# Whole token rows scattered into the experts' order, in place of a table of row numbers and gathers

## The chip, the cores and the metric

The kernel runs on one core of a Trainium2 chip. The metric is the device time of one execution in microseconds (us), median of several runs; for the kernel before it is 893.01 us (three runs: 884.34, 893.01, 897.72). Profiles come from one profiled execution each; TensorE is PE, VectorE is DVE, ScalarE is ACT, GpSimd is POOL, SyncE is SP.

## The reference

Attention, then a layer of eight experts. `q`, `k`, `v` are 8 batches x 8 heads x 576 tokens x 64. `q` and `k` are rotated, scores are scaled and go through a softmax, and the attention output is laid out as `x`, 4608 token rows of 512 values. Each token goes to one expert:

```
logits = x @ w_gate + modality_bias[modality_id]
e_idx = np.argmax(logits, axis=1)
gate_w = softmax(logits)[e_idx]
for e in range(8):
    mask = e_idx == e
    h = np.maximum(x[mask] @ w1[e], 0.0)          # 512 -> 1024
    out[mask] = gate_w[mask, None] * (h @ w2[e])  # 1024 -> 512
```

How many tokens an expert gets is known only when the kernel runs, so the rows of one expert have to be brought together.

## The kernel before, in words

**Attention** works on 32 pairs of heads (`NPAIR`), four pairs to a batch, b = n // 4 for pair n. For a pair the rotation takes four steps on POOL (`rope_`, parts 1, 0, 2, 4: lines 454 to 462) and one on ACT (part 3, which writes the high part), `swap` copies the halves of a head past each other with DMAs (L470), `scores`, `rowmin`, `expo`, `fill`, `evac`, `AV` and `outp` follow on PE, DVE and ACT. `load` brings the next q and k of a pair, 576 KB in each half, into one of two buffers.

**Routing.** After each fourth pair `xout` writes the batch's rows into `X` in DRAM, and `route` finds each token's expert, its gate and its place among the expert's tokens (`oi`). `scatter` (L727) then writes 8 bytes per token, its number and its gate (`VAL`), into the table `TAB` at row `oi`: five indirect DMAs of up to 128 rows a batch, issued by POOL.

**Experts.** Tokens are worked on in blocks of one expert: block 0 of 256 rows, eight superblocks of 512, one block of 256 and one of 128 (`slots`, `nt`), and up to 19 further blocks behind a branch. The first five blocks are planned from the first five batches alone (`plan0`, on POOL, during attention), the others from all eight (`plan`, on DVE, in small steps between those of superblocks 1 to 5, lists `POPS` and `late`). For a block `m_plan` reads expert and first row into SP's registers, `m_ix` loads the block's piece of the table twice (`ix` for the outputs, `xi` for the rows), and `m_gather` computes row numbers `iy` (L1000) and gathers the rows: one indirect DMA (L1013) brings 128 pieces of 512 bytes, so a superblock takes 16 and the whole run 148, all issued by POOL. Rows lie in four buffers `XG`, two of which are the memory of attention's `AT`. DVE transposes them (`m_tr`, L1058), `m_super` computes a superblock with seven products in place of eight (L1194), then the second layer (L1326), and `m_store` scatters the output rows (L1109). First weights come with `m_load1` (L1029), second with `m_load2` (L1034), on SP's queue; `m_split` and `m_wsplit` split them into a high and a low part.

**Order.** PE, ACT, DVE and POOL follow an order written out by hand: every step of attention has a key in `KEYS`, in units of us, which is added to 14.438 times the pair's number; `EDGE` gives other keys for single pairs, and `MOE` those of block 0 and of the first rows. Steps are issued in the order of their keys, each engine waits in that order for what it needs, and SP's queue keeps it as well until key `end` of the last pair (472.56). After that SP's order is set by the framework's scheduler, by when it expects things to be ready, and the other engines follow the program.

Of the kernel before, what the change touches and what calls it, by code (L numbers as in the profile page):

```python
# [18 lines left out]
P = 128  # L19
# [3 lines left out]
BLK = 256  # L23
# [5 lines left out]
NB_STATIC = 1  # L29

# [191 lines left out]
    rows=(5.189, -7.595, 2.778, 1.17, -0.984, 8.071, 5.429, 11.766, 15.341, 15.3411, 15.3412, 15.3413, 15.3414, 15.3415, 15.3416, 15.3417, 15.3418, 15.3419, 15.342, 15.3421, 15.3422, 15.3423, 15.3424, 15.3425),  # L222
# [3 lines left out]
AFTER = {(0, 3): (30, 'av', 0), (0, 4): (30, 'av', 0), (0, 5): (30, 'av', 1), (0, 6): (30, 'av', 1), (0, 7): (30, 'out', 1), (1, 0): (31, 'av', 0)}  # L226
# [4 lines left out]
def tile_attention_moe(ctx: ExitStack, tc: tile.TileContext, qk, v, mod, wg, mb, w1, w2, rope, cf, ci, out):  # L231
# [7 lines left out]
    X = dram.tile([N, DM], F32, name="X")  # L239
    TAB = dram.tile([(E + 1) * N, 2], I32, name="TAB")  # L240
# [11 lines left out]
    TOT = cst.tile([1, 1], I32, name="TOT")  # L252
    EPS = cst.tile([P, 1], F32, name="EPS")
# [111 lines left out]
    MI = rc.tile([P, B, 5, 2], I32, name="MI")  # L365
    WGT = rc.tile([P, DM // P, E], F32, name="WGT")
    MF = rc.tile([P, B, 5], F32, name="MF")
    BI = rc.tile([P, B, 5, E], F32, name="BI")
    MBB = rc.tile([P, 2, E], F32, name="MBB")
# [8 lines left out]
    def setup():  # L378
# [20 lines left out]
        TI = W1[0].rearrange("p a b -> p (a b)")[:, 0:(E + 1) * N * 2 // P].bitcast(I32)  # L399
        g.memset(TI, EMPTY)  # L400
        for t in XG[0:2]:
            g.memset(t, 0.0)
# [6 lines left out]
    def setdma(part):  # L409
# [10 lines left out]
        else:  # L420
            d(out=MBB.rearrange("p a e -> p (a e)"), in_=mb.rearrange("a e -> (a e)").unsqueeze(0).to_broadcast([P, 2 * E]))
            d(out=TAB.rearrange("(p r) w -> p (r w)", p=P), in_=TI)

    def setup2(part):
# [8 lines left out]
        else:  # L433
            BT = sm.tile([P, B * 5, E], F32, name="BT", tag="BT", bufs=1)
# [188 lines left out]
    def xout(b):  # L623
        Bt = bt_[b]
        xd = X[b * S:(b + 1) * S, :]
        nc.sync.dma_start(out=xd[0:512, :].rearrange("(p j) d -> p j d", j=4), in_=Bt["x"])
# [3 lines left out]


# [92 lines left out]
    def scatter(b, j):  # L724
# [3 lines left out]
            out=TAB, out_offset=bass.IndirectOffsetOnAxis(ap=oi[0:n, j:j + 1], axis=0),  # L728
            in_=VAL[0:n, b, j, :], in_offset=None, bounds_check=E * N - 1, oob_is_err=False).ins
# [7 lines left out]


# [5 lines left out]
    def plan0():  # L744
# [44 lines left out]
        cmp = t1("cmp", [NB_MAX, E])[:, 0:NSA + 1, :]  # L789
# [17 lines left out]
        G_.tensor_scalar(ge, nb, -float(SUP), float(N), op0=ALU.mult, op1=ALU.add)  # L807
        G_.tensor_tensor(cs, cs, ge.unsqueeze(1).to_broadcast(shs), op=ALU.mult)
        G_.tensor_tensor(hc, hc, EBv, op=ALU.add)
        G_.tensor_scalar(hc, hc, float(-E * N), None, op0=ALU.add)  # L810
# [4 lines left out]
        G_.tensor_scalar(rb[:, 0:1], rb[:, 0:1], float(E * N), None, op0=ALU.add)  # L815
# [3 lines left out]
        G_.tensor_copy(PLA[:, 1, 0:NA], rb)  # L819
# [5 lines left out]
        G_.tensor_scalar(EB9, sl[:, 0:E + 1], float(N), None, op0=ALU.mult)  # L825
        G_.tensor_scalar(EBN, EBv, float(-E * N), None, op0=ALU.add)
# [3 lines left out]
    def plan():  # L830
# [26 lines left out]
        def blocks(x, n, w, o, eo):  # L857
# [15 lines left out]
            V_.scalar_tensor_tensor(o[:, 1, 0:n], sl[:, 0:n], float(w), rb[:, 0:n], op0=ALU.mult, op1=ALU.add)  # L873
# [39 lines left out]
        yield  # L913
        V_.tensor_reduce(hr, hc, op=ALU.add, axis=AX.X)
        yield
        V_.tensor_scalar(pl[:, 1, ns:ns + 1], hr, float(E * N), None, op0=ALU.add)
# [778 lines left out]
```

## Time and profile before

| | |
|---|---|
| median of three runs | 893.01 us |
| profiled execution, time and span | 888.49 and 886.6 us |
| PE busy | 838.3 us, 95% of the span |
| DVE, ACT, POOL busy | 725.3, 622.3, 649.0 us |
| moved by DMA | 141.06 MB, 159 GB/s over the span |
| mean granted TensorE clock | 0.988 |

The span runs from the first to the last instruction. Attention fills it up to about 465 us, the experts the rest. A row of the table by stage gives the busy time of each engine in that stretch, the granted clock, the mean busy share of the 16 DMA engines, and their rate. Busy time of PE is modelled from pipelined matmuls; what counts here is its idle time and who ended it.

### The profile page before, as it was taken

What the parts mean: (1) busy time and instruction counts of PE and PEld (TensorE: products, weight loads), DVE (VectorE), ACT (ScalarE), POOL (GpSimd) and SP (SyncE); (2) the same over time, 40 slices, a digit from 0 to 9 for tenths busy, and PEclk for the clock granted to TensorE, in tenths of its full rate; (3) what the DMA queues carried; (4) which work ended last, traced back from release to release, by engine and by line L of the source; (5) the groups of instructions that cost most, each with busy time, mean ns of one, the idle gap of its engine ahead of it and who ended that gap; (6) DMA issues with size and microseconds to landing.
All of it is one profiled execution on the core that took longest, in us unless ns stands there. A gap on an engine that the chain in (4) does not pass through costs nothing.

```text
span 886.6 us, 24920 instructions
## 1 busy us (share of the span) xinstructions
PE 838.3 (95%) x9504; PEld 690.8 (78%) x9504; DVE 725.3 (82%) x1612; ACT 622.3 (70%) x1325; POOL 649.0 (73%) x507
## 2 busy tenths in 40 slices
PE   2899999999999999999989799999999998999995
PEld 2687777777777777777768689898989896989895
DVE  6788888898898988888878788989988986798562
ACT  2897989889898888887964467565646563646453
POOL 3899988988989989999358888886886865334111
PEclk9999999999999999999999999999999998999999
DMA  8766868878788786755847292244445321521330
GB/s 266 222 191 169 265 171 213 175 202 207 193 204 195 201 202 173 223 153 155 228 126 237 86 187 74 78 128 159 159 143 185 109 73 34 167 86 52 113 140 22
DMA packets 84346, 141.06 MB, mean 159 GB/s; under 512 B 27592, under 2 KB 54364, under 8 KB 83192
## 3 DMA queue, kind: packets, MB, share of 16 engines
q1 hardware_dynamic: 73624, 118.28, 49.2%
q0 software_dynamic: 9248, 19.46, 7.0%
q8 instruction: 77, 1.26, 0.6%
q10 hardware_dynamic: 1344, 1.62, 0.6%
q14 instruction: 53, 0.43, 0.2%
HBM read 104.61 MB, written 19.51 MB: 140 GB/s over the span
## 4 chain that ended last, share of the span: by engine, by line
PE 79%; DVE 7%; issue 5%; ACT 4%; POOL 4%; DMA 1%; POOLq 0%; SPq 0%; DVEq 0%; ACTq 0%
PE psY L1326 18%; PE ps L566 16%; PE ps L485 14%; PE psH L1194 12%; PE ps L508 9%; PE ps L601 3%; PE psY L1194 2%; PE ps L1079 1%; PE psH L1079 1%; PE psY L1098 1%; ACT P L503 1%; DVE X L1155 1%; POOL HL L462 1%; DVE W1L L442 1%; DMA SW<-HL 1%
## 5 line engine op out<-in xcount | busy, mean ns | idle before, releaser
L494 DVE CUSTOM_DVE_ANT_1 sc<-ps,ZERO 128x576 f32<-128x576 f32 x288 | 206.6, 749 | 24.8 <-PE ps L485 14.6
L503 ACT ACTIVATE P<-sc,mn 128x576 f32<-128x576 f32 x256 | 196.0, 769 | 5.7 <-DVE mn L494 5.1
L485 PE MATMUL ps<-HL 64*128 64x288 f32 x960 | 170.9, 312 | 14.9 <-ACT HL L445 10.7
L485 PE MATMUL ps<-SW 64*128 64x288 f32 x960 | 170.4, 313 | 5.8 <-DMA SW<-HL 5.6
L485 PEld LDWEIGHTS ps<-HL 64*128 64x128 f32 x960 | 136.5, 191 | 20.7 <-ACT HL L445 10.7
L485 PEld LDWEIGHTS ps<-SW 64*128 64x128 f32 x960 | 136.3, 191 | 10.2 <-issue 7.7
L566 PE MATMUL ps<-PH,AT 128*64 128x320 f32 (+1 forms) x1024 | 139.3, 414 | 2.1 <-DVE PH L541 1.9
L1194 PE MATMUL psH<-HL,W1H 128*128 128x256 f32 x576 | 123.3, 283 | 5.8 <-ACT TB L445 3.0
L1013 POOL DMA_INDIRECT XG<-X,iy x80 | 106.9, 1336 | 29.7 <-issue 20.7
L541 DVE COPY PH<-ps 128x512 f32<-128x512 f32 (+1 forms) x160 | 98.4, 631 | 14.3 <-PE ps L508 8.5
L445 ACT ACTIVATE PH<-ps 128x512 f32<-128x512 f32 (+1 forms) x160 | 85.3, 551 | 33.1 <-PE ps L508 23.1
L566 PEld LDWEIGHTS ps<-PH,AT 128*64 128x64 f32 x1024 | 68.3, 137 | 51.1 <-DVE PH L541 5.3
L1194 PE MATMUL psH<-HL,W1L 128*128 128x256 f32 x384 | 107.9, 281 | 0.0
L462 POOL TENSOR_TENSOR HL<-ST,HL 128x1152 fp32r<-128x1152 f32 x31 | 82.4, 2657 | 34.3 <-ACT HL L445 34.2
L508 PEld LDWEIGHTS ps<-idf,P 64*128 64x128 f32 x2304 | 86.7, 138 | 21.7 <-ACT P L503 9.2
L1326 PE MATMUL psY<-W2H,SW 128*128 128x512 f32 x256 | 102.0, 399 | 1.5 <-issue 1.5
L1013 POOL DMA_INDIRECT AT<-X,iy x68 | 88.2, 1297 | 20.4 <-issue 18.3
L1326 PE MATMUL psY<-W2L,SW 128*128 128x512 f32 x256 | 101.5, 396 | 0.7 <-issue 0.7
L508 PE MATMUL ps<-idf,P 64*128 64x64 f32 x2304 | 98.2, 225 | 3.7 <-ACT AT L445 1.6
L1194 PEld LDWEIGHTS psH<-HL,W1H 128*128 128x128 f32 x576 | 96.1, 190 | 7.1 <-ACT TB L445 3.2
L1109 POOL DMA_INDIRECT out_dram<-sc,ix x36 | 41.8, 1162 | 68.7 <-ACT sc L1108 60.6
L458 POOL TENSOR_TENSOR ST<-ST 128x1152 f32<-128x1152 f32 x30 | 79.6, 2653 | 1.2
(281 smaller groups left out, 1984.7 us busy)
## 6 DMA issues: line engine op xcount, KB each, us to landing
ST<-in_moe_w_dram SPq DMA_DIRECT2D x88, 512.0 KB
ST<-in_qk_dram SPq DMA_DIRECT2D x62, 576.0 KB
SW<-HL SPq DMA_DIRECT2D x124, 216.0 KB
AT<-in_v_dram SPq DMA_DIRECT2D x32, 256.0 KB
X<-X SPq DMA_DIRECT2D x8, 1024.0 KB
XG<-X,iy POOLq DMA_INDIRECT x80
AT<-X,iy POOLq DMA_INDIRECT x68
AT<-in_v_dram SPq DMA_DIRECT2D x64, 16.0 KB
```

Source lines behind the costliest of these rows:

```text
L445: return nc.scalar.activation(o, i, AF.Copy, scale=scale)
L458: e.tensor_tensor(a, a, b, op=ALU.add)
L462: e.tensor_tensor(d["HL"][:, 1, o], a, d["HL"][:, 0, o].bitcast(F32), op=ALU.subtract)
L485: nc.tensor.matmul(ps[:, g, 0:288], t[:, wq, q0:q0 + P], t[:, wk, k0:k0 + 288], start=(m == 0), stop=(m == len(L) - 1))
L494: nc.vector.tensor_tensor_reduce(sc, d.pop(("S", u))[:, :, 0:288], ZERO.unsqueeze(2).to_broadcast([P, 2, 288]), 1.0, FMAX, ALU.add, ALU.mi ...
L503: nc.scalar.activation(p, sc.rearrange("p a b -> p (a b)"), AF.Exp, bias=mn, scale=-1.0, accum_out=d["sum"][:, u:u + 1])
L508: nc.tensor.transpose(ps[:, g, c:c + 64], src[r, k0:k0 + P], idf[r, r])
L541: alone(d["at", f], g, (nc.vector.tensor_copy if g else acopy)(o, i).ins, int(f[1] in "23B"))
L566: i = nc.tensor.matmul(pa[hh * 64:hh * 64 + 64, 0:c1 - c0], d["V"][:, hh, kt, :], r, start=(kt == 0), stop=(kt == 4))
L1013: inst = nc.gpsimd.indirect_dma_start(out=x[:, t, g, :], out_offset=None, in_=X.rearrange("n (i f) -> (n i) f", f=P)[0:rows], in_offset=ba ...
L1194: nc.tensor.matmul(ps[b][:, r * BLK:r * BLK + BLK], w[:, c, f0:f0 + P], x[:, c, :], start=(first and r == 0 and c == 0 and i == 0), stop=( ...
L1326: nc.tensor.matmul(po[t], hx[:, c, o:o + P], w[:, c, :], start=(k == 0 and c == 2 * q and i == 0), stop=(k == 3 and c == 2 * q + 1 and i = ...
```

## The change

`X` rows get longer: 512 values, then token number and gate, in a pitch of 528 words. `vout` writes numbers and gates of a batch there, `back` loads 128 whole rows into one of two buffers `XL`, and `scatter` writes these whole rows to their place in `XS`, a DRAM array with room for each expert (`RS` rows) in which the experts' rows lie in order. `TAB`, the index arithmetic and all 148 gathers go; a block's rows are now plain transfers of `XS` on SP's queue, four for each 256 rows (`m_rows`), and `m_ix` is a single load of numbers and gates. `pads` writes a block of empty rows behind each expert's last row, once all tokens are counted, since a block may reach past them. `ZR` holds these empty rows; the tail of `XS` is filled at the start, as `TAB` was. Constants of routing move into memory of the `XG` buffers, the clearing of `XG` at the start and by ACT falls away, and in `plan` the first row of a block is limited with one more small instruction. Keys: the late places of the scatters of batches 4, 5 and 6 (pairs 19, 23 and 27) are dropped for those in `KEYS`, and `vout` and `back` get keys of their own, on SP's queue for batches 0 to 5 and on POOL's for 6 and 7.

```diff
+RS = N + BLK
+XW = DM + 16
+XU = DM + 2
...
-    "RK8": 55.05, ..., "RK14": 74.22, "SC0": 76.39, "SC1": 91.58,
+    "RK8": 55.05, ..., "RK14": 74.22, "VO": 69.0, "BK0": 71.4, "BK1": 71.5, "BK2": 90.0, "BK3": 101.0, "BK4": 114.0, "SC0": 76.39, "SC1": 91.58,
     "SC2": 105.27, "SC3": 118.91, "SC4": 121.32,
...
     19: {
-        "SC3": 113.825, "SC2": 128.215, "SC4": 152.075,
     },
     23: {
-        "RK6": 45.016, "RK7": 49.391, "RK8": 52.824, "RK9": 58.16, "RK10": 79.988, "RK11": 109.721, "RK12": 128.347, "RK13": 128.956,
-        "RK14": 129.684, "SC3": 130.859, "SC4": 132.359, "SC2": 132.942, "SC1": 136.961, "SC0": 137.506,
     },
...
     27: {
+        "VO": 82.49, "BK0": 82.53, "BK1": 82.54,
...
-    rows=(5.189, -7.595, 2.778, 1.17, -0.984, 8.071, 5.429, 11.766, 15.341, ...),
+    rows=(-13.5, 11.7, 20.6, 31.756, 31.757),
...
-    X = dram.tile([N, DM], F32, name="X")
-    TAB = dram.tile([(E + 1) * N, 2], I32, name="TAB")
+    X = dram.tile([N, XW], F32, name="X")
+    XS = dram.tile([E * RS + SUP, XW], F32, name="XS")
+    ZR = dram.tile([BLK, XU], F32, name="ZR")
...
-            d(out=TAB.rearrange("(p r) w -> p (r w)", p=P), in_=TI)
+            for i in range(2):
+                d(out=ZR[i * P:i * P + P, :], in_=TI)
+            d(out=XS[E * RS:E * RS + SUP, 0:XU].rearrange("(p r) w -> p r w", r=4), in_=TI.unsqueeze(1).to_broadcast([P, 4, XU]))
...
+    def vout(b, eng=nc.sync):
+        xd = X[b * S:(b + 1) * S, DM:XU]
+        eng.dma_start(out=xd[0:512, :].rearrange("(p j) w -> p j w", j=4), in_=VAL[:, b, 0:4, :].bitcast(F32))
+        eng.dma_start(out=xd[512:576, :], in_=VAL[0:64, b, 4, :].bitcast(F32))
...
         inst = nc.gpsimd.indirect_dma_start(
-            out=TAB, out_offset=bass.IndirectOffsetOnAxis(ap=oi[0:n, j:j + 1], axis=0),
-            in_=VAL[0:n, b, j, :], in_offset=None, bounds_check=E * N - 1, oob_is_err=False).ins
+            out=XS, out_offset=bass.IndirectOffsetOnAxis(ap=oi[0:n, j:j + 1], axis=0),
+            in_=xl[b, j][0:n], in_offset=None, bounds_check=E * RS - 1, oob_is_err=False).ins
...
+    def back(b, j, eng=nc.sync):
+        t = xl[b, j] = XL[len(xl) % 2]
+        xd = X[b * S:(b + 1) * S, 0:XU]
+        if j < 4:
+            eng.dma_start(out=t[:, 0:XU], in_=xd[0:512, :].rearrange("(p j) w -> j p w", j=4)[j])
+        else:
+            eng.dma_start(out=t[0:64, 0:XU], in_=xd[512:576, :])
+
+    def pads():
+        nc.vector.tensor_copy(CNT, RUN[0:1, B, :])
+        for e in range(E):
+            r = nc.sync.value_load(CNT[0:1, e:e + 1], min_val=0, max_val=E * RS - BLK)
+            inst = nc.sync.dma_start(out=XS[bass.ds(r, BLK), 0:XU], in_=ZR[:, :]).ins
...
-        xi = d["xi"] = ixp.tile([P, 16, 2], I32, name="xi", tag="xi")
-        tab = TAB[bass.ds(d["r"], k * P), :]
...
-        i1 = nc.sync.dma_start(out=ix[:, 0:k, :], in_=rows).ins
-        i2 = nc.sync.dma_start(out=xi[:, 0:4 * k, :], in_=tab.rearrange("(q g) w -> q (g w)", g=4 * k).unsqueeze(0).to_broadcast([4, 32, 8 * k])).ins
+        tab = XS[bass.ds(d["r"], k * P), DM:XU].rearrange("(q a g) w -> g q a w", a=k, g=4)
+        m_taken(s, nc.sync.dma_start(out=ix[:, 0:k, :].bitcast(F32), in_=tab).ins)
...
-    def m_gather(s, j, t, g, after=None):
...
-        inst = nc.gpsimd.indirect_dma_start(out=x[:, t, g, :], out_offset=None,
-                                            in_=X.rearrange("n (i f) -> (n i) f", f=P)[0:rows],
-                                            in_offset=bass.IndirectOffsetOnAxis(ap=d["iy"][:, c:c + 1], axis=0),
-                                            bounds_check=rows - 1, oob_is_err=False)
...
+        rows = XS[bass.ds(d["r"], nt[s] * P), 0:DM].rearrange("(q r) (i f) -> i q r f", r=n, i=4)[:, :, 8 * j:8 * j + min(n, 8)]
+        x = rows_of(s, j).rearrange("p t g f -> p (t g) f")[:, 0:min(n, 8)]
+        for i in range(4):
+            m_taken(s, nc.sync.dma_start(out=x[32 * i:32 * i + 32], in_=rows[i]).ins)
...
-                late = steps + [(lambda: [f(*a) for f, *a in scats],)] + [(each, next) + ((planned, None),) * 4] * 13
+                late = steps + [(lambda: [vout(B - 1, nc.gpsimd)] + [(back(B - 1, j, nc.gpsimd), scatter(B - 1, j)) for j in range(5)] + [pads()],)] + [(each, next) + ((planned, None),) * 4] * 13
                 continue
...
+            eng = nc.sync if n // 4 < B - 2 else nc.gpsimd
+            K_("VO", vout, n // 4, eng)
             for i, x in enumerate(scats):
+                K_(f"BK{i}", back, n // 4, i, eng)
                 K_(f"SC{i}", *x)
```

## Rows read from the trace of the kernel before

**Rows 1.** The page's first part: busy us, share of the span, instructions.

```profile
PE 838.3 (95%) x9504; PEld 690.8 (78%) x9504; DVE 725.3 (82%) x1612; ACT 622.3 (70%) x1325; POOL 649.0 (73%) x507
```

**Rows 2.** Busy time by stage: stretch, its length, busy us (instructions), clock, DMA share, GB/s.

```profile
0.00:30.00 30.00, 11.57 (x119) 9.42 (x121) 22.04 (x55) 12.01 (x26) 16.35 (x26) 0.99 0.89 269
120.00:420.00 300.00, 293.44 (x4790) 223.96 (x4788) 256.20 (x765) 262.13 (x674) 273.10 (x204) 1.00 0.77 192
420.00:545.00 125.00, 115.67 (x1126) 95.88 (x1123) 103.06 (x193) 77.91 (x152) 85.82 (x78) 0.97 0.60 164
545.00:720.00 175.00, 174.27 (x1118) 156.96 (x1117) 156.76 (x247) 104.74 (x156) 135.34 (x103) 1.00 0.40 131
...
760.00:887.00 127.00, 117.37 (x741) 104.94 (x739) 81.04 (x96) 67.66 (x95) 32.19 (x29) 0.98 0.29 97
```

**Rows 3.** Chain that ended last, 340 to 430: start us, us, what.

```profile
405.17 1.09 POOL TAB L727
...
409.04 2.65 POOL ST L458
...
413.25 1.71 PE ps L508 x48
```

**Rows 4.** Timeline of ACT near 412: start, us, instruction, idle before it.

```profile
411.71 1.16 ACT L445 ACTIVATE HL<-ST 128x1152 fp32r<-128x1152 f32 x1 [3.26 <-POOL ST L458]
```

**Rows 5.** Timeline of DVE near 490.

```profile
487.29 1.22 DVE L1155 TENSOR_TENSOR X<-ST 128x1024 f32<-128x1024 f32 x1 [0.24 <-DMA X<-X]
...
489.69 0.70 DVE L1058 STREAM_TRANSPOSE AT<-AT 128x512 f32<-128x512 f32 x1
493.70 0.71 DVE L1058 STREAM_TRANSPOSE AT<-AT 128x512 f32<-128x512 f32 x1 [3.31 <-issue]
```

**Rows 6.** Timeline of POOL: the last of eight gathers for these rows.

```profile
486.46 1.46 POOL L1013 DMA_INDIRECT AT<-X,iy  x1 [0.30 <-issue]
```

**Rows 7.** Waits of PE, whole run: us in total, times, longest.

```profile
PE ps L485 <- DMA SW<-HL: 5.6, 2, 5.3
...
PE psH L1194 <- ACT HL L445: 2.1, 1, 2.1
```

**Rows 8.** A table read: issue on SP's queue, and POOL's instruction that waits for it.

```profile
435.24 0.61 SPq L982 DMA_DIRECT2D xi<-TAB  x1
...
437.74 0.27 POOL L1000 TENSOR_SCALAR iy<-xi,CF 128x8 int32<-128x8 int32 x1 [8.07 <-DMA xi<-TAB]
```

**Rows 9.** Waits of SP's queue, whole run.

```profile
SPq L1029 <- DVE X L1155: 140.5, 8, 23.4
```

**Rows 10.** Busy time from 505 to 510, columns as in rows 2.

```profile
505.00:510.00 5.00, 2.77 (x13) 2.77 (x14) 5.00 (x7) 2.66 (x5) 4.23 (x3) 0.72 0.15 43
```

**Rows 11.** Lines 727 and 1109: duration ns min/median/max, first and last start.

```profile
L727 POOL DMA_INDIRECT TAB<-VAL,oi x40: 911/1048/2021, 130.5 to 599.0; - x40
...
L1109 POOL DMA_INDIRECT out_dram<-sc,ix x36: 982/1024/1781, 522.9 to 865.8; - x36
```

**Rows 12.** Timeline of POOL: batch 4's last scatter.

```profile
422.39 0.94 POOL L727 DMA_INDIRECT TAB<-VAL,oi  x1 [0.15 <-issue]
```

**Rows 13.** Batch 1's routing: swaps on SP's queue, and its first scatter on POOL.

```profile
179.03 3.83 SPq L470 DMA_DIRECT2D SW<-HL  x4
...
184.75 1.02 POOL L727 DMA_INDIRECT TAB<-VAL,oi  x1 [0.28 <-DMA SW<-HL]
```

**Rows 14.** Waits of POOL, 50 to 430.

```profile
POOL HL L462 <- ACT HL L445: 18.7, 16, 3.4
```

**Rows 15.** The page's third part: packets, MB, share of 16 engines.

```profile
q1 hardware_dynamic: 73624, 118.28, 49.2%
q0 software_dynamic: 9248, 19.46, 7.0%
```

**Rows 16.** First weights of superblock 4: issue on SP's queue, ACT's first use.

```profile
584.74 8.96 SPq L1029 DMA_DIRECT2D ST<-in_moe_w_dram  x4
...
608.93 1.05 ACT L445 ACTIVATE W1H<-ST 128x1024 fp32r<-128x1024 f32 x1
```

More of the change, by code (lines that the diff above doesn't have):

```diff
@@ L252, in tile_attention_moe @@
     TOT = cst.tile([1, 1], I32, name="TOT")
+    CNT = cst.tile([1, E], I32, name="CNT")
+    XL = [cst.tile([P, XW], F32, name=f"XL{i}") for i in range(2)]
     EPS = cst.tile([P, 1], F32, name="EPS")
@@ L398, in setup @@
         nonlocal TI
[L399 to L402, printed above, removed]
+        TI = XG[0].rearrange("p t g f -> p (t g f)")[:, 0:XU]
+        g.memset(TI, 0.0)
+        for x in XL:
+            g.memset(x[:, XU:XW], 0.0)
+        g.memset(TI[:, DM:DM + 1].bitcast(I32), EMPTY)
         g.memset(ON, 1.0)
@@ L736, in scatter @@
                 tc.declare_no_dep(inst, x, reason="the first plan's blocks lie before the rows of later batches")
+    xl = {}
+    def back(b, j, eng=nc.sync):
[10 more added lines that the diff above has]
+            inst = nc.sync.dma_start(out=XS[bass.ds(r, BLK), 0:XU], in_=ZR[:, :]).ins
+            for _b, x in placed:
+                tc.declare_no_dep(inst, x, reason="rows behind those of the tokens")
+            for x in taken:
+                tc.declare_no_dep(inst, x, reason="the first plan's blocks are full")
+            placed.append((B, inst))
     AB9, EB9, CP9 = (cst.tile([1, E + 1], F32, name=n) for n in ("AB9", "EB9", "CP9"))
@@ L915, in plan @@
         yield
-        V_.tensor_scalar(pl[:, 1, ns:ns + 1], hr, float(E * N), None, op0=ALU.add)
+        V_.tensor_scalar(pl[:, 1, ns:ns + 1], hr, float(E * RS), None, op0=ALU.add)
         yield
@@ L982, in m_ix @@
-        i2 = nc.sync.dma_start(out=xi[:, 0:4 * k, :], in_=tab.rearrange("(q g) w -> q (g w)", g=4 * k).unsqueeze(0).to_broadcast([4, 32, 8 * k])).ins
-        if not slots[s][0]:
-            for i in (i1, i2):
-                for b, x in placed:
-                    if b >= NPL:
-                        tc.declare_no_dep(i, x, reason="the first plan's blocks lie before the rows of later batches")
-                    else:
-                        tc.add_manual_dep(i, x.name, mybir.DependencyInfo(mybir.DependencyClass.Sync, mybir.DependencyReason.DATA),
-                                          reason="the table's rows of the first plan's batches")
-                taken.append(i)
@@ L1022, in m_rows, with m_taken @@
-    def m_rows(s, j=0):
-        for t in halves(s):
-            for g in range(4):
-                m_gather(s, j, t, g)
+        tab = XS[bass.ds(d["r"], k * P), DM:XU].rearrange("(q a g) w -> g q a w", a=k, g=4)
+        m_taken(s, nc.sync.dma_start(out=ix[:, 0:k, :].bitcast(F32), in_=tab).ins)
+    def m_taken(s, i):
+        if slots[s][0]:
+            return
+        for b, x in placed:
+            if b >= NPL:
+                tc.declare_no_dep(i, x, reason="the first plan's blocks lie before the rows of later batches")
+            else:
+                tc.add_manual_dep(i, x.name, mybir.DependencyInfo(mybir.DependencyClass.Sync, mybir.DependencyReason.DATA),
+                                  reason="the table's rows of the first plan's batches")
+        taken.append(i)
@@ L1598 @@
 CF_W = 0
-for _n, _w in (("U", P), ("EB", E), ("W8", E), ("I4", 1), ("TRI", E * E), ("SL", NB_MAX)):
+for _n, _w in (("U", P), ("EB", E), ("W8", E), ("TRI", E * E), ("SL", NB_MAX)):
     CF_OFF[_n] = (CF_W, _w)
```

75 lines of the change are left out of this document (26 added, 49 removed), and 2 rows, old and new, of the table KEYS.

## The prediction

> **What bounds the kernel now.** I read the page's first part and then its stretches: TensorE (PE) is busy for 838.3 of 886.6 us [rows 1]. So 48.3 us are idle, and the table by stage says where [rows 2]: 18.4 in the first 30 us, before there is work for it; 6.6 of the 300 us of attention from 120 to 420; 9.3 around the change from attention to the experts (420 to 545); 0.7 of the 175 us from 545 to 720, where PE is simply full; 9.2 after 760, mostly the last output. The change leaves the start and the last output alone. What is left to win is 48.3 - 18.4 - 9.2 = 20.7 us, 2.3% of the span, and only part of it belongs to gathers.
>
> Two places matter. The first is the end of attention. The chain of waits there runs on POOL, over a scatter and two steps of the rotation, and then back to PE [rows 3]; ScalarE, which works in a fixed order, stood 3.26 us behind that last POOL step [rows 4]. So here a microsecond on POOL ahead of 409 is a microsecond of the kernel. The second is the first expert superblock: VectorE transposes the first half of the second 512 KB of rows at 489.69 and the next half only at 493.70, after 3.31 us idle that the view leaves unnamed [rows 5]. The last of the eight gathers for that half started at 486.46 and took POOL 1.46 us [rows 6], so I read the idle time as waiting for it to land. PE then waits 2.1 us for ScalarE's split of these rows [rows 7].
>
> **The change, part by part.**
>
> *Gathers to plain transfers.* 148 gathers go (8 for block 0, 16 for each of eight superblocks, 8 and 4 at the end), with the index arithmetic before them. 76 transfers on SP's queue take their place (4 for each of 19 half blocks), and the 22 small table reads become 11. POOL is not what PE waits for between 545 and 720 (0.7 us idle), so nothing comes back there. On SP, 76 issues at the 0.61 us of a table read [rows 8] are 46 us, set against 140.5 us in which SP waits for VectorE before it can load first weights at all [rows 9]: hidden. If that cover were gone, a superblock would pay 8 x 0.61 = 4.9 us. At 490 it is different: the rows' four transfers are ordered at key 468, 21 us before the transpose. The 3.3 us go. What is late next is the copy-out of the last batch's X: VectorE's weight sum already waited 0.24 us for it at 487.29 [rows 5], and new row transfers now share the engines with it. Bounds: nothing back (X slips by as much), or 3.3 plus the low clock behind it: the stretch 505 to 510 was granted 0.72, between the two levels of 2.4 and 1.2 GHz, after PE's waits [rows 10], which costs 5 x 0.28 = 1.4 us. I take -3.3, because the transposes' idle time is the row that shows the wait itself.
>
> The Trainium skill (TensorE: Matmul & The Clock Gate, "Part 1: The HAM clock gate") says that the clock falls to half behind an idle array and comes back with work. By that rule the term would be -4.7; the sum does without it.
>
> *Scatters of whole rows.* There are 40 as before. A scatter of 8 B rows costs POOL 1048 ns in the median, one of 2 KB rows (the outputs) 1024 [rows 11]: no change on POOL. What does change is their place. Batch 4's last scatter ran at 422.39 [rows 12]; its key falls from 426.4 to 395.6 (19 x 14.438 + 121.32), ahead of the POOL step of key 409.07 that ends the chain at 409.04. Batch 5's first goes from key 469.6 to 408.5, also ahead of it; two routing steps of batch 5, of one small operation each, go with it and are counted as nothing. That is 2 x (1.05 + 0.15) = 2.4 us more on POOL before 409, where ScalarE and PE wait for POOL. Bounds: 0 if the late steps find other slack, +5 if the scatter also waits 2.5 us for its rows. I take +2.4, since ScalarE's 3.26 us there [rows 4] say that the slack is gone.
>
> *vout and back, new.* Per batch there are two small stores and five loads; batches 0 to 5 issue them on SP, 6 and 7 on POOL. The first load waits for the stores to land and the first scatter for that load. The nearest row for a round trip is a table read: issued at 435.24, it let POOL start at 437.74, 2.5 us [rows 8]. In batch 1 the first two swaps stand at 179.03 (four took 3.83, the last two behind POOL's step) [rows 13]. Behind two of them (1.2, at 0.61 an issue), two stores (1.2), a landing (2.5), a load (0.6) and its landing (2.5) it is 187.0, while the scatter ran at 184.75 [rows 13]: POOL waits some 2.3 us per batch. What covers it is that POOL already waits for ScalarE, 18.7 us in 16 waits between 50 and 430 [rows 14]; a late POOL first eats those. Behind the waiting load on SP stand two swaps and the next q/k loads, 3 us later. PE waited for swaps only 5.6 us in the whole run, in two waits [rows 7], and all its idle time from 120 to 420 is 6.6. I take 0; the uncovered price is the first rival. Of batches 6 and 7 nobody needs the rows before the second plan's first block: hidden behind at least a superblock.
>
> *DMA traffic.* Back and scatter add 576 x (2056 + 2112) B = 2.4 MB a batch, 14.4 MB for six batches. POOL's queue moved 19.46 MB in 7.0% of the span, 314 GB/s; SP's 118.28 MB in 49.2%, 271 GB/s [rows 15]. So it takes 46 to 53 us of all 16 engines. From 120 to 420 they were busy 0.77 of 300 us [rows 2], which leaves 69: they go to 92 or 95%. The 8 B stores of vout replace as many 8 B pieces of the scatters. I take 0, since it fits.
>
> The Trainium skill (DMA: Bandwidth & Descriptors, "Issuing engines are not separate DMA queues") states that transfers of SP and POOL run on the same engines and interleave. It speaks against the change: moving rows to SP would save issue time alone, and the added bytes would delay swaps and loads. By it this term would be above nothing, as in the first rival.
>
> *pads.* Eight DRAM to DRAM copies of 526 KB, 4.2 MB, 13 to 16 us at the rates above, and up to 31 if reading and writing both count. They stand behind the last routing step, in the third quarter of superblock 2's second layer, by the order of the steps about when the first weights of superblock 4 are issued (584.74, 8.96 us long; my estimate); ScalarE first uses those at 608.93 [rows 16]. Cover: 608.93 - 593.70 = 15 us if the copies go first, all of it if they go behind. Bounds 0 to +16; I take 0.
>
> *The rest.* The larger fill at the start (1.6 MB in place of 0.3) and POOL's shorter clearing come before anything reads them; one more DVE instruction in the plan and two clears less on ACT lie beside a full PE: nothing, and uncovered no more than an instruction each.
>
> **The sum.** -3.3 + 2.4 = -0.9 us on a profiled execution of 888.49 (886.6 and 1.9 around it), which is 887.6. That execution is 0.5% below the median shown, 893.01, so against the median I say 892: no change.
>
> **Rivals.** *Slower: SP and the DMA engines in attention.* Each batch puts 7 issues (4.2 us) and one landing (2.5) on SP ahead of swaps and loads, on engines that are 92% full or more. If all 6.7 us were uncovered, six batches cost 40; half of it costs 20, which is 912 beside the forecast. It decides once a batch's lateness is more than POOL's waits for ScalarE in its four pairs (18.7 / 16 x 4 = 4.7 us), or once the added bytes move below 14.4 MB / 69 us = 209 GB/s. For it: the fixed order and the narrow margin. Against it: the swaps cost PE nothing in mid-attention now. Chance 0.15.
>
> *A few us faster.* The clock comes back too and the late POOL steps find slack: -4.7 against the median is 888. For it: PE's wait of 2.1 behind the same rows [rows 7] and the low clock after it [rows 10]. Chance 0.2.
>
> *A few us slower.* Pads or X's copy-out take the gather's place as what is late: no -3.3, and +5 from pads or the q/k loads: 893 + 2.4 + 5 = 900. Chance 0.2.
>
> *Over 2% faster* would need 18 of the 20.7 us, when the gathers explain about 5. Chance 0.05.
>
> The forecast itself (within 4 us of 892) has 0.4.
>
> **Range and chances.** The lowest run shown is 884.34, and the best sum, -4.7, with that spread gives 883; upwards the few-us rival and part of the SP rival give 908. 2% is 18 us, about what a measurement of this kernel can tell from no change (the three runs spread over 13). Faster 0.05; slower 0.15 from SP and 0.01 from pads at their bound; within 2% the rest, 0.79.
>
> **What would show it.** Right: the transposes' idle time near 490 is gone; ScalarE's wait on POOL near 412 grows to some 5 us; PE stays full from 545 to 720; the DMA share of 120 to 420 is 0.9 or a little more. Wrong: PE or POOL waiting on swaps or q/k loads in mid-attention; VectorE waiting near 487 on X's copy-out; ScalarE waiting near 609 for first weights; or ScalarE's wait near 412 unchanged, which would say that the moved scatters found slack.

## The result, and the profile after

The changed kernel takes 889.06 us (median of 18 runs, 885.48 to 892.32) against 884.24 for the kernel before (18 runs too; the 893.01 shown ahead is the middle of three of them). The ratio is 1.0052, 95% interval 1.0030 to 1.0074: 4.6 us slower, less than 2%, but not nothing. The ratio leaves out two runs of the kernel before, 893.01 and 897.72, which lie over 1.5% above its fastest and count as slow. In a later job the kernel before took 875.47 and the kernel after 886.04, ratio 1.0126 (1.0101 to 1.0151). So the loss is 4.6 to 11 us, and it is the kernel before that varies more from job to job (884.24 against 875.47, the kernel after 889.06 against 886.04).

The profiled execution of the kernel after took 888.06 us, its span 886.3; against 888.49 and 886.6 nothing seems to have happened. But the span hides two changes that cancel. First the page's busy times, which answer to [rows 1]:

```profile
PE 833.8 (94%) x9504; PEld 687.3 (78%) x9504; DVE 725.2 (82%) x1615; ACT 619.3 (70%) x1323; POOL 456.6 (52%) x365
```

POOL lost 192 us of work and 142 instructions, and PE is nearly as busy as before. Then the table by stage, columns as in [rows 2]:

```profile
0.00:30.00 30.00, 11.67 (x135) 9.50 (x137) 22.34 (x56) 12.66 (x27) 14.84 (x27) 1.00 0.90 272
...
120.00:420.00 300.00, 289.81 (x4688) 220.39 (x4688) 252.52 (x754) 256.35 (x658) 269.19 (x206) 0.99 0.80 231
420.00:545.00 125.00, 119.52 (x1237) 100.40 (x1234) 108.90 (x207) 82.67 (x165) 36.04 (x36) 0.99 0.72 211
545.00:720.00 175.00, 174.47 (x1116) 157.08 (x1116) 156.07 (x247) 105.37 (x157) 32.20 (x29) 1.00 0.56 161
720.00:760.00 40.00, 40.00 (x249) 35.69 (x248) 33.99 (x45) 23.02 (x35) 5.19 (x4) 1.00 0.32 83
760.00:887.00 127.00, 108.38 (x662) 95.88 (x660) 74.96 (x88) 60.02 (x84) 13.45 (x14) 0.94 0.26 85
```

PE lost 3.6 us from 120 to 420, won 3.9 from 420 to 545, and is full from 720 to 760, where it stood 4.0 us in the kernel before:

```profile
720.00:760.00 40.00, 36.05 (x189) 29.82 (x188) 30.05 (x39) 18.91 (x27) 23.36 (x20) 0.91 0.15 46
```

So after 760 it has 9.0 us less left to do, and the span ends where it did. The end is where to look. These are the last two long instructions of POOL in each kernel, the semaphore step `INC_SWDGE_SEM`, at the branch for the further blocks, and the drain `DRAIN`, where the program closes (line, engine, name, count, shortest/middle/longest in ns, first and last start in us); first the kernel before, behind its last output scatter, which started at 879.04:

```profile
L1591 POOLq INC_SWDGE_SEM  x1: 700/700/700, 882.9 to 882.9; - x1
...
L1691 POOLq DRAIN  x3: 46/109/2118, 883.6 to 886.3; - x3
```

and of the kernel after, its last output scatter in POOL's timeline (start, us, instruction, idle before it):

```profile
870.06 0.98 POOL L1376 DMA_INDIRECT out_dram<-sc,ho  x1 [0.43 <-issue]
```

and its step and drain, with SP's drains beside them:

```profile
L1596 POOLq INC_SWDGE_SEM  x1: 2200/2200/2200, 875.0 to 875.0; - x1
...
L1695 SPq DRAIN  x3: 7/7/13, 877.9 to 885.7; - x3
...
L1695 POOLq DRAIN  x3: 46/109/8241, 877.2 to 886.0; - x3
```

The output has been issued at 871.0, 9 us earlier than before (880.0). But the step takes 2.20 us in place of 0.70 and the drain 8.24 in place of 2.12: 10.44 against 2.82, 7.6 us more. The stretch in which the drain runs, columns as in the table by stage, is empty on every engine and every DMA engine:

```profile
874.00:886.00 12.00, 0.00 (x0) 0.00 (x0) 0.00 (x0) 0.00 (x0) 0.00 (x0) 0.50 0.00 0
```

Neither instruction counts as busy, so the page's list of costly groups doesn't show them.

To see the rest, take the same ScalarE instruction in two traces and subtract its starts (after minus before, us). The three columns are pairs of traces: the first two profiles, a second profile of the kernel before against the first of after, and a pair from the faster jobs (the kernel before with 16 small stores more, and the third profile of after, both below).

| near, us | first pair | before again | faster pair |
|---|---|---|---|
| 100 | -1.9 | -0.3 | -0.8 |
| 340 | -1.9 | -1.4 | -1.8 |
| 350 | -2.2 | -0.4 | -1.7 |
| 370 | +1.1 | +2.2 | -0.8 |
| 410 | +4.1 | +5.2 | +2.4 |
| 440 | +5.1 | +5.4 | +2.7 |
| 472 | +0.5 | -0.9 | +2.7 |
| 502 | -2.5 | -3.2 | -0.3 |
| 720 | -3.4 | -2.9 | +0.4 |
| 860 | -9.0 | -2.6 | +1.1 |

Every pair loses 4.6 to 7.0 us between 340 and 440 and wins 2.3 to 3.1 between 472 and 502; two of three win back most of the loss before 472, because the kernel before stalls there (rows below). So in the second and third pair compute ends 2.6 us earlier and 1.1 later, and the end adds 7.6. With the second pair that is 5.0 us, with the third 8.7, beside the measured 4.6 and 10.6.

### The profile page after: what moved, and what is told of

The parts are those of the page before. It is cut to its first block, busy times and chain, and to the rows that moved or that the text cites. A ratio compares the mean times of both kernels' runs of the same rounds, so it can differ in the third digit from the quotient of the medians.

```text
span 886.3 us, 24877 instructions
## 1 busy us (share of the span) xinstructions
PE 833.8 (94%) x9504; PEld 687.3 (78%) x9504; DVE 725.2 (82%) x1615; ACT 619.3 (70%) x1323; POOL 456.6 (52%) x365
## 4 chain that ended last, share of the span: by engine, by line
PE 72%; DVE 7%; POOL 7%; DMA 4%; issue 4%; ACT 3%; POOLq 0%; SPq 0%; DVEq 0%; ACTq 0%
PE psY L1331 18%; PE ps L573 14%; PE psH L1199 12%; PE ps L492 12%; PE ps L515 8%; PE ps L608 2%; DMA SW<-HL 2%; PE psY L1199 2%; POOL HL L469 1%; PE psH L1084 1%; PE psY L1103 1%; POOL ST L463 1%; POOL ST L465 1%; DVE X L1160 1%; DVE W1L L449 1%
## 5 line engine op out<-in xcount | busy, mean ns | idle before, releaser
L492 PE MATMUL ps<-HL 64*128 64x288 f32 x960 | 168.6, 309 | 13.8 <-ACT HL L452 11.2
L492 PE MATMUL ps<-SW 64*128 64x288 f32 x960 | 168.1, 309 | 6.2 <-DMA SW<-HL 5.5
L1114 POOL DMA_INDIRECT out_dram<-sc,ix x36 | 46.5, 1291 | 230.8 <-ACT sc L1113 224.4
L492 PEld LDWEIGHTS ps<-HL 64*128 64x128 f32 x960 | 134.3, 187 | 19.7 <-ACT HL L452 11.2
L492 PEld LDWEIGHTS ps<-SW 64*128 64x128 f32 x960 | 133.7, 187 | 11.0 <-DVE ST L463 4.8
L738 POOL DMA_INDIRECT XS<-XL,oi x40 | 45.0, 1125 | 64.3 <-DMA XL<-X 42.9
L1199 PEld LDWEIGHTS psH<-HL,W1L 128*128 128x128 f32 x384 | 72.7, 189 | 0.0
```

Source lines behind the costliest of these rows:

```text
L492: nc.tensor.matmul(ps[:, g, 0:288], t[:, wq, q0:q0 + P], t[:, wk, k0:k0 + 288], start=(m == 0), stop=(m == len(L) - 1))
L1114: inst = nc.gpsimd.indirect_dma_start(out=out, out_offset=bass.IndirectOffsetOnAxis(ap=d["ix"][:, t, 0:1], axis=0), in_=y, in_offset=None, ...
L1199: nc.tensor.matmul(ps[b][:, r * BLK:r * BLK + BLK], w[:, c, f0:f0 + P], x[:, c, :], start=(first and r == 0 and c == 0 and i == 0), stop=( ...
```

## The experiments

### The same kernels again

**e1_before_again**, the kernel before without an edit.

> The kernel before once more, unchanged, for a second profile. In the first profile ScalarE stood 3.7 and 1.3 us near 732 and 736 with nothing named that PE waited for, the granted clock fell to half behind it, and 5.8 us were lost there against the kernel after; POOL's last long drain took 2.1 us. Theory A (the stall belongs to the gathers, which POOL was issuing at that moment): it is there again, within 3 us of the same place, and the profiled execution takes some 888 us. Theory B (the stall is an accident of that execution): it is absent, the last output scatter ends about 6 us earlier, at 874 in place of 880, and the execution takes about 883. On the end: if the drain's length is an accident it differs from 2.1 us by several us; if it belongs to the kernel it is 2 to 3 us.

It took 882.41 us, its span 880.5. The stall near 732 is gone, one near 446 is there, and the drain is 2.118 us once more. Rows of ScalarE, of the first trace of before:

```profile
447.59 0.60 ACT L445 ACTIVATE PH<-ps 128x512 f32<-128x512 f32 x1 [2.69 <-PE ps L485]
...
736.30 0.60 ACT L1200 ACTIVATE SW<-psH 128x512 fp32r<-128x512 f32 x1 [3.72 <-remote]
```

and of the second:

```profile
448.97 0.60 ACT L445 ACTIVATE PH<-ps 128x512 f32<-128x512 f32 x1 [4.48 <-remote]
...
730.29 1.07 ACT L1200 ACTIVATE SW<-psH 128x512 fp32r<-128x512 f32 x2
```

Theory B holds for 732 (an accident), and the drain belongs to the kernel. "remote" says that the profile names no engine and no queue of this core; what these stalls wait for stays open. By the starts behind them, set against a profile without them (e6 below), each cost 5 to 7 us, with the low clock that followed, and that is most of what lies between these executions of the kernel before. From 440 to 465 (columns as in the table by stage) e1 had

```profile
440.00:465.00 25.00, 20.58 (x346) 15.01 (x342) 17.21 (x47) 16.53 (x42) 11.58 (x19) 0.93 0.42 128
```

and the kernel before with 16 small transfers more, all of them issued later than this (e6 below), was full:

```profile
440.00:465.00 25.00, 25.00 (x392) 19.45 (x383) 23.71 (x58) 20.80 (x47) 16.93 (x21) 1.00 0.56 175
```

The stall near 446 is no accident of e1 alone. It is in the first profile too, and in those of e4 and e11 (PE busy for 20.1 and 22.2 of these 25 us, clock 0.93). These four come from jobs in which the kernel before takes 880.79 to 884.24 us, e6 from one in which it takes 875.48.

**e2_after_again**, the kernel after without an edit.

> The kernel after once more, unchanged, for a second profile. In the first one compute ends 9 us earlier than before (last output scatter ends at 871 against 880), but 15.3 us lie between that scatter's end and the span's end, against 6.6 before: POOL waits 3.5 us more and its drain takes 8.2 us in place of 2.1. Theory A (the long end belongs to the changed kernel): 13 to 17 us again. Theory B (accident): 6 to 9 us, and the execution takes about 880. On the late attention: if the half clock at 364 to 368, which cost about 2 us, is an accident, POOL's last rotation step that ScalarE waits for starts at about 411 in place of 413.1.

It took 887.38 us, span 885.6; step 2.200 and drain 8.241 us to the nanosecond, last output scatter at 870.30. Theory A. The half clock at 364 was an accident, but ScalarE's instruction behind POOL's last rotation step starts at 415.53, only 0.25 us earlier, and ScalarE still waited 3.48 us for it.

**e15_after_timed**, the kernel after again, beside e12 to e14.

> The kernel after, unchanged, beside the three others on the same chip. Theory: ratio to before 1.003 to 1.010 (the kernel before has differed between chips by 8 us in its median, the kernel after less), step 2.200 and drain 8.241 us for the third time.

886.04 us, ratio 1.0126 (1.0101 to 1.0151), a little over what was expected, with the kernel before at 875.47; step and drain 2.200 and 8.241 a third time.

### What makes the end long

**e5_last_two_on_sp**

```diff
-                late = steps + [(lambda: [vout(B - 1, nc.gpsimd)] + [(back(B - 1, j, nc.gpsimd), scatter(B - 1, j)) for j in range(5)] + ...
+                late = steps + [(lambda: [vout(B - 1)] + [(back(B - 1, j), scatter(B - 1, j)) for j in range(5)] + ...
...
-            eng = nc.sync if n // 4 < B - 2 else nc.gpsimd
+            eng = nc.sync
```

> The kernel after with vout and back of batches 6 and 7 issued by SP in place of POOL: 14 plain transfers less on POOL's queue (8 left of 22; the kernel before has 6). In four profiles so far POOL's long drain at the end took 2.118 us in every execution of a kernel with 6 plain POOL transfers and 8.241 us in every one with 22, and the semaphore step ahead of it 0.700 and 2.200 us. Theory (both grow with the plain transfers that POOL issues, whenever it does): by the straight line through these two points the drain is 2.9 us and the step 0.9, the end is 6.7 us shorter, and the kernel takes 882 to 883 beside 881 for before (ratio to before 0.998 to 1.001). Rival 1 (the length of the end goes with the size of scattered rows or the number of indirect transfers, 78 against 226): drain and step stay at 8.2 and 2.2. Rival 2 (SP pays): the end is shorter, but SP waits for value stores and scatters with first weights queued behind it, and 3 to 10 us are lost between 470 and 620.

884.76 us, ratio 1.0110 (1.0082 to 1.0138): step 1.916, drain 7.097. All three expectations miss: 14 plain transfers less shorten the end by 1.4 us, not 6.7, but they do shorten it. That is 0.020 + 0.082 us for each. What the third feared, a loss on SP's queue, does not show in the time.

**e6_plain_in_before**

```diff
+        if 1 <= s <= 4:
+            nc.gpsimd.dma_start(out=DT[t % 2], in_=cf[:, 0:8])
```

> The kernel before with 16 small plain transfers more on POOL's queue (4 KB each, from a constant into a spare tile, one behind each output scatter of superblocks 1 to 4; nothing reads them): 22 in all, as in the kernel after. Theory: step 2.200 and drain 8.241 us as in the kernel after, 7.6 us more at the end and nowhere else, ratio to before 1.0086 or a little less. Rival 1 (the rows' size or the number of indirect transfers): 0.700 and 2.118 as before, time the same. Rival 2 (bytes or packets of these transfers): the drain grows by well under 1 us, since 16 x 4 KB is 6% of the 1.0 MB that the kernel after writes at its start alone.

877.10 us against 875.48, ratio 1.0014 (0.9993 to 1.0035). The two rows at its end:

```profile
L1594 POOLq INC_SWDGE_SEM  x1: 1020/1020/1020, 869.5 to 869.5; - x1
...
L1694 POOLq DRAIN  x3: 46/109/3425, 870.6 to 874.6; - x3
```

16 transfers add 0.32 and 1.31 us: the same 0.020 and 0.082 each, on another kernel and for 4 KB in place of 257. So it is the number of transfers, not their bytes, and 6.0 of the 7.6 us are not the plain ones.

**e7_no_vout**

```diff
+        nc.gpsimd.tensor_copy(xl[b, j][0:n, DM:XU].bitcast(I32), VAL[0:n, b, j, :])
...
+        if eng is nc.gpsimd:
...
+            eng.indirect_dma_start(out=t[0:n, 0:DM], out_offset=None, in_=X[0:(b + 1) * S, :],
+                                   in_offset=bass.IndirectOffsetOnAxis(ap=VAL[0:n, b, j, 0:1], axis=0), ...)
```

> The kernel after without vout: X holds values of x alone, POOL copies number and gate (128x2) into XL right ahead of each scatter, and back of batches 6 and 7 is an indirect load in place of a plain one. 8 plain POOL transfers are left of 22. Theory: step and drain as in the run with batches 6 and 7 on SP (some 0.9 and 2.9 us), 6.7 us back at the end. In attention the landing of vout leaves the way to the first scatter of a batch (X stores land long before), so POOL's waits of 11.7 us on row loads fall to under 4, against 40 copies of 0.2 us on POOL, 30 of them in attention: between 1 us lost and 2 us won there. Sum: ratio to before 0.996 to 1.000. Rival (POOL's waits were covered anyway and its work is not): 30 x 0.2 = 6 us on POOL, 1 to 3 us lost in late attention, ratio 1.000 to 1.003.

884.13 us, ratio 1.0100 (1.0075 to 1.0125): step 2.116, drain 7.914. Against e5 it has ten indirect loads more and 0.20 and 0.82 us more: an indirect transfer counts like a plain one. From 340 to 470 it was 3 to 6 us ahead of e2 by ScalarE's starts, and it lost 4.2 near 620, where ScalarE waited 6.1 us for output scatters (1.4 in e2) that stood behind batch 7's on POOL.

So far: the steps of the kernels with 86, 96 and 100 POOL transfers lie on a line, 0.200 + 0.020 us a transfer, so these pay for all of them, and the kernel before, with 232, for (0.700 - 0.200) / 0.020 = 25. As if something had cleared 207 on the way.

**e8_112_more**

```diff
+        for i in range(28 if t == 3 and 4 <= s <= 7 else 0):
+            nc.gpsimd.dma_start(out=DD[28 * (s - 4) + i], in_=CF[:, 0:8])
```

> The kernel after with 112 small stores more on POOL's queue (4 KB each from a constant into a DRAM array that nothing reads; 28 behind the last output scatter of each of superblocks 4 to 7, where POOL is idle some 35 us): 212 transfers by POOL in all. The runs so far: kernels with 100, 96 and 86 POOL transfers of any kind end with a semaphore step of 2.200, 2.116 and 1.916 us and a drain of 8.241, 7.914 and 7.097 us, that is 0.0200 and 0.0817 us a transfer; those with 232 and 248 end with 0.700 and 2.118, and 1.020 and 3.425 us, the same slopes for 25 and 41 transfers. Theory (the end clears up what is left since the last clearing, and one clearing came after 207 transfers): 5 are left, step 0.30 and drain 0.48 us, the end is 9.6 us shorter than in the kernel after, ratio to before about 0.994 to 0.998. Rival (no clearing: the slope goes on): step 4.4, drain 17.4, 11.4 us more than the kernel after. Second rival (the 64 us of POOL's time are paid elsewhere): the drain is short, but scatters come late and PE waits.

878.97 us, ratio 0.9946 (0.9914 to 0.9978): 112 transfers that nobody needs make the kernel faster than the one before, in this job. Step 0.420, drain 0.972: 11 left, where 5 were expected.

**e9_50_more**, the same edit with 12, 12, 13 and 13 stores.

> The same with 50 stores more, 150 POOL transfers in all, fewer than 207. Theory: step 3.20 and drain 12.33 us, 5.1 us more than the kernel after. Rival (clearing comes earlier, by bytes, packets or time): less than in the kernel after.

883.15 us, ratio 0.9999 (0.9973 to 1.0025). The theory said 3.20 and 12.33; the rows say 55 of 150 left:

```profile
L1599 POOLq INC_SWDGE_SEM  x1: 1290/1290/1290, 878.4 to 878.4; - x1
...
L1698 POOLq DRAIN  x3: 46/109/4566, 879.7 to 884.8; - x3
```

**e11_before_204**

```diff
+        if s in (8, 9, 10):
+            return
         rows = (N if slots[s][0] else NPL * S) * 4
```

> The kernel before without the 28 gathers of the last superblock and of the two blocks behind it (their rows are left as the buffers hold them, so outputs of these blocks are not the reference's; every other instruction stays): 204 POOL transfers, just under 207. Theory: nothing is cleared before the end, step 4.3 and drain 16.7 us in place of 0.7 and 2.1, so 18 us more at the end: ratio to before 1.018 to 1.021, though the kernel does less. Rival (fewer gathers, less to clear up): step and drain as before or shorter, ratio 0.998 to 1.000.

891.11 us, ratio 1.0084 (1.0057 to 1.0112): slower by 7.4 us with 28 gathers less. Step 2.275, drain 8.570, 104 left and not 204:

```profile
L1693 POOLq DRAIN  x3: 46/109/8570, 885.7 to 894.9; - x3
```

Both misses say the same: a clearing comes not after 207 transfers but after about every hundred.

**e12_10_more**, as e8 with 3, 3, 2 and 2 stores.

> The kernel after with only 10 small stores more on POOL's queue (two or three behind superblocks 4 to 7), 110 transfers in all. Theory (a clearing about every hundred transfers; the kernel after ends just short of one): 3 to 15 transfers are left, step 0.3 to 0.5 us, drain 0.3 to 1.3 us, the end 8.6 to 9.9 us shorter than in the kernel after, as with 112 more. Rival (the clearing in the run with 112 came from their bytes or from POOL's 64 us): 110 are left, step 2.4, drain 9.06 us, 1 us more than the kernel after.

877.23 us against 886.04 for the kernel after in the same job: 8.8 us for ten stores of 4 KB, 8.6 of them in the step and the drain. Ratio to before 1.0019 (1.0001 to 1.0037).

```profile
L1599 POOLq INC_SWDGE_SEM  x1: 496/496/496, 873.3 to 873.3; - x1
...
L1698 POOLq DRAIN  x3: 46/109/1299, 873.8 to 875.7; - x3
```

All together (left = (step - 0.200) / 0.020; the drain gives the same by (drain - 0.07) / 0.0817):

| kernel | POOL transfers | step, us | drain, us | left |
|---|---|---|---|---|
| e5 | 86 | 1.916 | 7.097 | 86 |
| e7, e14 | 96 | 2.116, 2.120 | 7.914 | 96 |
| after (three profiles), e3 | 100 | 2.200 | 8.241 | 100 |
| e12 / e13 | 110 | 0.496 / 0.420 | 1.299 / 0.972 | 15 / 11 |
| e9 | 150 | 1.290 | 4.566 | 55 |
| e11 | 204 | 2.275 | 8.570 | 104 |
| e8, e10 | 212 | 0.420 | 0.972 | 11 |
| before (two profiles), e4 | 232 | 0.700 | 2.118 | 25 |
| e6 | 248 | 1.020 | 3.425 | 41 |

A saw: the end grows by 0.10 us a transfer up to about a hundred and falls back. The kernel after stands at its tip. Cleared are 95 to 100, or 201 to 207, which would be two goes. No row shows a clearing; that there is one is read from these numbers, and what sets it off, and what it costs when it comes, stays open.

### Late attention

**e4_early**

```diff
     19: {
-        "SC3": 113.825, "SC2": 128.215, "SC4": 152.075,
     },
     23: {
-        "RK6": 45.016, ..., "SC0": 137.506,
     },
```

> The kernel before with one part of the change alone: the late keys of batches 4 and 5 dropped, so that two or more scatters (of 8 B rows, no loads of rows) move ahead of POOL's step at 409. Theory of the prediction: POOL's step of 409.03 starts 2.4 us later, ScalarE's wait on it grows from 3.3 to some 5 us, and the kernel takes up to 2.4 us more (ratio to before up to 1.003). Rival (POOL's lateness is eaten by slack at the end of attention, where the kernel after won back 4.6 us between 440 and 465): the step moves but the time is the same within 1 us.

889.58 us against 880.79, ratio 1.0093 (1.0064 to 1.0122): some 8 us, over three times the most that the theory allowed. In its trace, taken from the slowest of its six executions (894.04), ScalarE waits 3.90 us behind the POOL step that it waited 3.25 us for in e1:

```profile
418.50 1.16 ACT L442 ACTIVATE HL<-ST 128x1152 fp32r<-128x1152 f32 x1 [3.90 <-POOL ST L455]
```

The start is 7.9 us later than e1's 410.61, but 4.5 of that were lost before 340, ahead of any edit. By ScalarE's starts the lag stays as it is from 340 to 370 and grows by 3.4 us from there to 410, where the early scatters stand. From 340 to 472 it grows by 6.6 us, with a granted clock of 0.53 or 0.54 three times (from 394, 448 and 469; in e1 once, 0.57 from 451). Batch 5's scatters now stand between the gathers on POOL (458.15, 463.79). That the early keys cost more than POOL's 2.4 us is shown; what the rest behind 410 is made of is not.

**e3_late5**

```diff
     23: {
+        "RK13": 128.956, "RK14": 129.684, "SC0": 130.859, "SC1": 132.359, "BK2": 132.4, "SC2": 134.4, "BK3": 134.5, "SC3": 136.961, "BK4": 137.0, "SC4": 138.5,
     },
```

> The kernel after with the late keys of batch 5's last routing steps and scatters as before (463 to 471 in place of 408 to 455). Theory of the prediction (POOL ahead of 409 is the chain): one scatter of 1.1 us and 0.4 us of routing leave the chain, ScalarE's wait behind POOL's last rotation step falls from 4.0 to about 2.5 us, and the kernel takes 1 to 2 us less than the kernel after (ratio to before 1.003 to 1.004). Rival (the loss in late attention comes from landings of value stores, row loads and swaps on SP's queue, of which this moves only the four loads of one batch): POOL's last step moves by less than 0.5 us or the time is unchanged within 0.5 us. Second rival: the scatters now stand between batch 6's stores and the first expert rows, and 1 to 3 us are lost near 470.

886.72 us, ratio 1.0074 (1.0046 to 1.0102), beside one run of the kernel after at 887.38 in the same job. ScalarE's wait fell from 3.48 to 2.45 us, as the theory said:

```profile
413.41 1.17 ACT L453 ACTIVATE HL<-ST 128x1152 fp32r<-128x1152 f32 x1 [2.45 <-POOL ST L466]
```

The time is within a microsecond of that one run, which can't tell the theory's 1 to 2 us from nothing. In the traces e3 is 4.0 us ahead of e2 at 472 and 1.7 from 550 on. That these keys are worth little in the changed kernel is better shown by e10 beside e8, below.

**e14_no_vout_alone**, X without numbers and gates, POOL copies them into XL (as in e7), back of batches 6 and 7 plain.

> The kernel after without vout alone (back of batches 6 and 7 stays plain, 96 POOL transfers). Theory (vout's landing holds POOL up in late attention): 1 to 4 us less than the kernel after before 470, 0.4 us less at the end (step 2.12, drain 7.91). Rival (what it holds up is given back by 460 anyway): no more than the 0.4 us of the end.

885.28 us, ratio 1.0113 (1.0089 to 1.0137), 0.8 us less than e15, 0.4 of it at the end as the rows of step and drain have it. POOL's waits for row loads fell from 11.7 to 1.9 us; in their place it waited 7.8 us for its own copies (the scatter L734 behind the copy L733) and 1.0 us more for ScalarE. Waits of POOL from 50 to 430 (us in total, times, longest), of e14:

```profile
POOL HL L469 <- ACT HL L452: 8.6, 9, 2.8
POOL XS L734 <- POOL XL L733: 7.8, 26, 0.6
```

against e15:

```profile
POOL XS L738 <- DMA XL<-X: 11.7, 5, 3.0
POOL HL L469 <- ACT HL L452: 7.6, 5, 3.0
```

By ScalarE's starts e14 is 3.4 us ahead of e15 at 410 and 0.4 at 472. The rival: what vout's landing holds up is given back by 460. How much the copies take of what the landing gave, this run does not separate.

### Versions that put it together

**e10_best**, the edits of e3 and e8.

> The kernel after with both repairs: the late keys of batch 5 as before, and 112 small stores on POOL's queue. Theory: the end 9.6 us shorter and 1 to 2 us from late attention: some 11 us below the kernel after, ratio to before 0.992 to 0.996. Rival: the gains do not add, ratio 0.998 or more.

878.82 us against 883.67, ratio 0.9932 (0.9905 to 0.9959), as expected; next to e8's 0.9946 the keys add nothing that can be told.

**e13_best_of**, the edits of e3 and e14, and 14 stores.

> The kernel after without vout (X holds x alone, POOL copies number and gate into XL ahead of each scatter, back stays plain), with the late keys of batch 5 as before and 14 small stores on POOL's queue, 110 transfers in all. Theory: end 9 us shorter, 1 us from the keys and 1 to 4 us from vout's landing: 11 to 14 us below the kernel after, ratio to before 0.990 to 0.993. Rival: the copies cost POOL in late attention what the landing gave, ratio 0.994 or more.

877.50 us against 875.47, ratio 1.0016 (0.9998 to 1.0033); e12 had 1.0019. The rival: without the long end the kernel is 8.5 us faster than the kernel after, and nothing in attention adds to it. Against the kernel before these versions win 0.5 to 0.7% in the job where it takes 883.67 us (e8, e10) and nothing where it takes 875.47 (e12, e13).

## Why the prediction was wrong

It said no change, -0.9 us on the profiled execution; the change costs 4.6 us, in another job 11. That the 889.06 us measured lie near the 892 forecast is luck: the 892 started from 893.01, and the kernel before takes 884.24. By its steps:

- **The step that failed** is "The change leaves the start and the last output alone", with "so nothing comes back there" of the gathers on POOL between 545 and 720. The last output's work is untouched, but the end behind it is not: 232 POOL transfers became 100, and by the table of the saw that left 100 to clear up in place of 25. 75 x (0.020 + 0.0817) = 7.6 us, the measured 10.44 - 2.82. No row of the kernel before was read for its end; the 2.1 us of drain were in its trace, though that they go by a count shows only beside other kernels. This term alone turns -0.9 into +6.7, and ten stores that take it away (e12) gave 8.8 us back.
- **-3.3 us at the transposes** was right in mechanism. The idle time [rows 5] is gone; the two halves follow each other without a gap (row x2), and what was named as late next is: VectorE waits 1.31 us for X's copy-out, before 0.24. Columns as in [rows 5], of the kernel after:

```profile
488.21 1.23 DVE L1160 TENSOR_TENSOR X<-ST 128x1024 f32<-128x1024 f32 x1 [1.31 <-DMA X<-X]
...
490.61 1.30 DVE L1063 STREAM_TRANSPOSE AT<-AT 128x512 f32<-128x512 f32 x2
```

  The table of starts gives 2.3 to 3.1 us between 472 and 502; 3.31 - 1.07 of idle time give 2.2. In e1, the kernel before again, the same idle time is 2.31 us and named: it waits for the gather, as was read.

```profile
494.37 0.71 DVE L1058 STREAM_TRANSPOSE AT<-AT 128x512 f32<-128x512 f32 x1 [2.31 <-DMA AT<-X,iy]
```

- **The clock** behind it did not come back: the stretch that answers to [rows 10] is granted 0.74, before 0.72. The Trainium skill (TensorE: Matmul & The Clock Gate, "Part 1: The HAM clock gate") has the clock come back with work; by that rule the term was -4.7. Here that stall went and the low clock stayed: PE was busy for 1.92 of the 5 us ahead of it (4.20 in the kernel before), so other gaps are left there, and the trace decides for the term without it.

```profile
500.00:505.00 5.00, 1.92 (x16) 1.72 (x15) 5.00 (x7) 3.89 (x7) 1.85 (x2) 0.92 0.32 109
505.00:510.00 5.00, 4.30 (x25) 4.09 (x26) 3.81 (x6) 2.47 (x5) 3.87 (x3) 0.74 0.32 67
```

- **+2.4 us for scatters ahead of 409** had the right sign. ScalarE's wait grew from 3.26 [rows 4] to 4.01 us (some 5 were forecast), and POOL's step starts at 413.10, before 409.03:

```profile
415.78 1.16 ACT L452 ACTIVATE HL<-ST 128x1152 fp32r<-128x1152 f32 x1 [4.01 <-POOL ST L465]
```

  The size was a little small: from 370 to 410 the three pairs lose 3.0, 3.0 and 3.2 us by ScalarE's starts, and e4, which has the early scatters and no row loads, 3.4. That is not all that late attention loses by 440, which is 4.6 to 7.0 us; the next term has a part of the rest. By 472 the loss is 2.4, 0.5 and 4.5 us in the three pairs: in the first two the kernel before loses much of it too, in its own stall near 446. That stall is visible in the trace of before (a clock of 0.91 from 445 to 450) and was not a term.
- **vout and back at 0** was right up to 340, and for the reason given: POOL's waits for row loads came, 11.7 us in 5 (2.3 a batch were forecast, 14 for six), and ate its waits for ScalarE, 6.8 us left of the 18.7 of [rows 14]: 18.5 together. The pairs lose nothing by 340. It was not right in batch 4: there the landings stand on the chain, where [rows 3] had none, and from 350 to 370 the pairs lose 3.3, 2.6 and 0.9 us, the first two with a granted clock of 0.57 from 364 to 368 in the trace of after, which e2 does not have.

```profile
341.79 3.96 DMA X<-VAL
345.80 2.58 DMA XL<-X
...
349.19 1.02 POOL XS L738
```

  Over the whole run the chain passes such landings in batches 1 and 4 of this trace (0, 3 and 4 in e2, 2, 3 and 4 in e15); what they cost ahead of 340 was covered.

  The rival of 912 did not happen: the stage 120 to 420 lost 3.6 us of PE, not 20. Of batches 6 and 7 "hidden" was right too, as far as rows go: it is their 14 transfers that are paid, 1.4 us at the end.
- **DMA traffic at 0** was right, its size was not: the share went from 0.77 to 0.80, not to 0.92, while the rate rose from 192 to 231 GB/s. 39 GB/s x 300 us are 11.7 MB in 9 us of all engines, where the queues' mean rates of 271 to 314 GB/s had given 37 to 43. In e1 and e6, whose attention is that of the kernel before, the share is 0.79, so it may be 3 us as well. The mean rates over the run were no price for these rows. PE waited 5.5 us for swaps in the whole run, before 5.6 [rows 7], so the added bytes did not delay those for it.
- **Pads at 0** held. The copies went ahead of three of the four weight transfers, and the weights' issue ends at 601.4, 7.7 us later than in [rows 16]; ScalarE waited 1.58 us and PE none.

```profile
583.73 10.82 SPq L764 DMA_DIRECT2D XS<-ZR  x8
594.87 6.54 SPq L1034 DMA_DIRECT2D ST<-in_moe_w_dram  x3
...
607.23 1.06 ACT L452 ACTIVATE W1H<-ST 128x1024 fp32r<-128x1024 f32 x1 [1.58 <-DMA ST<-in_moe_w_dram]
```

## What to carry to other kernels

Read the end of the span as a stage of its own: from the last output to the last instruction, sequencer rows included, in both kernels, before calling a change there "left alone". Work that is off the critical path can still be paid for at the end, by its count; here POOL's transfers, plain or indirect, cost 0.10 us each there, up to about a hundred. And profile the kernel before twice: a stall that is in one execution and not in the next is neither a gain to forecast nor a loss to explain.

## What was not expected of the hardware

POOL's last semaphore step and drain took 0.020 and 0.0817 us for every transfer by POOL that was left, to the nanosecond in repeated runs of the kernel before and of the kernel after, independent of size (4 to 257 KB) and kind, falling back after about each hundred (table above). The Trainium skill (VectorE: DVE Perf Modes, "The DRAIN you can't avoid") tells of drains from the preamble and postamble, constant at some 12 ns on all five engines. The drains here stand at the line of kernel.py where the program closes, so they need not be those: SP's, 7 to 13 ns, are of that size, POOL's longest, 0.97 to 8.57 us, are not, and the measurement decides.
